# Tile 3's first eight gate and val chunks as half-size products, and a new order of the statements, in an attention and SwiGLU kernel

## The chip, the core and the metric

The kernel runs on one core of a Trainium2 chip. TensorE (PE) multiplies into eight PSUM banks; VectorE (DVE), ScalarE (ACT) and GpSimd (POOL) work on what comes out; SyncE (SP) issues the DMAs. The metric is the device time of one execution in microseconds (us), as the median over runs. The profile of one execution gives the span from the first to the last instruction.

## What is computed

Decayed linear attention over 4 batches, 8 heads, 768 positions and a head size of 64, then a SwiGLU block on the 3072 tokens of width 512, with an inner width of 1536. Inputs and output are float32.

```python
for b in range(nb):
    intra = np.einsum('bhic,bhjc->bhij', qb, kb) * Dmask[None]
    intra = np.einsum('bhij,bhjd->bhid', intra, vb)
    inter = np.einsum('bhid,bhde->bhie', qb * lam_pow[None], kv_state)
    out[:, :, sl] = intra + inter
    kb_dec = kb * rev_pow[None]
    kv_state = lam_block[None, :, None, None] * kv_state + np.einsum('bhsd,bhse->bhde', kb_dec, vb)
...
g = x @ w_gate
silu = g * (1.0 / (1.0 + np.exp(-g)))
val = x @ w_val
return (silu * val @ w_out).astype(np.float32)
```

## The kernel before, in words

The tokens are cut into six tiles (t = 0 to 5) of 512 tokens, each made of two attention groups (g = 2t and 2t + 1) of 256 positions. Matrix products are in bfloat16 with float32 sums.

Attention of a group, in steps: the loads of k, q and v (`load_fp32`, on SP); the casts of k on ACT and the scaling of q on DVE, together `cast_scaled` (L287), which ends in a DMA transpose on SP into `qkt` (L279); the scaling of v (`v_scale`, L266); the scores on PE (L362, from group 6 on L392) and their masks on DVE (L369, L397); the state update `upd_mm` on PE (L424), the copies of its result on ACT (`upd_copy`, L446), and `state`, a chain of additions on POOL (L479) with casts to `kvn` (for groups 8 to 10 on ACT, L459 and L461, taken from a queue by `kv_flush`, L463); then `inter` (L518), a small `guard` copy on ACT, `intra` (L531), and two evacuations into the tile's x, `xt` (L544, L547). These products use 64 rows of the array.

The SwiGLU block of a tile has twelve chunks of 128 inner columns. A chunk (`ffn_fc`) is a gate of four products (L585) and a silu on ACT (L590), then a val of four products (L603) and a multiplication on DVE (L607) that gives the tile's h. Tiles 0 to 3 are done so, with 512 columns in a product, or in halves of 256 where the tile's second group is not there yet (one chunk of tile 0, all of tile 1, four chunks of tile 2).

Tiles 4 and 5 use half-size products in their gate and val instead: `ffn_unit` (L716) takes four chunks (two of each half of the inner width) for all 512 tokens as 2 x 2 blocks and makes them with seven products of blocks in place of eight, each product being four matmuls of 256 columns (L733). It needs sums of weight blocks (`w_combo`, L696), of x blocks (`x_combo`, L714), and copies and additions of partial results: two copies on ACT (L767, L770) and two additions on DVE (L775, L783) for each of gate and val. Four silu and four multiplications (one of them on POOL, L763) finish a unit. The output product does the same from tile 1 on: `out_units` (L805, matmuls L823) makes, with sums of h blocks (`h_combo`, L670) and of w_out blocks (`wo_combo`), two groups' rows in seven products of six matmuls each, called p1 to p7; tile 0 uses the plain `ffn_out` (L623).

The order of the work is what the order of calls in the program says: every engine works through its own queue in that order. Before, a planner writes it: `step` lists the chunks, `at` hangs calls behind a chunk, and the loop at L1184 runs the chunks one by one, between them `run_later` (masks put off), `drip` (one or two sums from the list `trickle`) and `kv_flush`. PSUM banks are taken in a ring by `bank`, unless `fixed` names them. Buffers come from pools with a fixed number of slots (ten of `raw`, three of `qk` and `qkt`, five of `h`, four of `osb`), each free again when its last reader is done.

Of the kernel before, what the change touches and what calls it, by code (L numbers as in the profile page):

```python
# [37 lines left out]
def _body(ctx, tc, nc, q, k, v, lam, moe_w_gate, moe_w_val, moe_w_out, out):  # L38
# [13 lines left out]

    NAT0 = 6
    NB = 4
# [212 lines left out]
    def load_group(g, parts="kqv"):  # L271
        for src, what in ((k, "kraw"), (q, "qraw"), (v, "v")):
            if what[0] in parts:
                load_fp32(g, nc.scalar if what == "kraw" and g in KACT else nc.sync, src, what)

    def dma_transpose(g):
        t = st[("qk", g)]
        tt = qkt_pool.tile([128, 2, 2, HP, 128], BF16, name="qkt", tag="qkt")
        nc.sync.dma_start(out=tt.rearrange("p a s h n -> p (a s h) n"),  # L279
                          in_=t.rearrange("p a s x -> p (a s x)"), transpose=True)  # L280
        st[("qkt", g)] = tt
        for put in held.pop(g, []):
            put()

    QP = ()

    def cast_scaled(g, eng=nc.vector):  # L287
        eng = nc.gpsimd if g in QP else eng
        t = qk_pool.tile([128, 2, 2, H * D], BF16, name="qk", tag="qk")
        st[("qk", g)] = t  # L290
        nc.scalar.copy(out=t[:, 0].rearrange("p s (h d) -> p h s d", h=H),
                       in_=st[("kraw", g)].rearrange("p h (s d) -> p h s d", s=2))
        eng.tensor_tensor(out=t[:, 1].rearrange("p s (h d) -> p h s d", h=H),
                                in0=st[("qraw", g)].rearrange("p h (s d) -> p h s d", s=2),
                                in1=qfac(g), op=ALU.mult)
        dma_transpose(g)
# [38 lines left out]
    KACT = ()  # L335
    HOLD = {(1, 1): 10}
    held = {}
# [6 lines left out]
    def scores(g, cs=(0, 1), warm=0):  # L344
# [9 lines left out]
        for c in cs:  # L354
# [12 lines left out]
            for h2 in range(2):  # L367
                def do_mask(c=c, h2=h2):
                    nc.vector.tensor_tensor(  # L369
                        out=ssb[:, h2, 2 * c:2 * c + 2].rearrange("p a s n -> p a (s n)"),  # L370
                        in0=sp[(c, h2)].rearrange("p (a x) -> p a x", a=2),
                        in1=bap(causal, [[0, 2], [1, 2 * BLK]]),
                        op=ALU.mult)
                later.append(do_mask)
# [5 lines left out]
    def scores_n(g):  # L380
# [14 lines left out]
        for h2 in range(2):  # L395
            def do_mask(h2=h2):
                nc.vector.tensor_tensor(out=ssb[:, h2], in0=sp[h2].rearrange("p (a x) -> p a x", x=M),  # L397
                                        in1=bap(causaln, [[0, 2 * HP], [1, M]]), op=ALU.mult)
            later.append(do_mask)

    def upd(g):
        upd_mm(g)
        upd_copy(g)
        state(g)
# [58 lines left out]
    def kv_flush(age=0, m=9):  # L463
        while kvq and m and len(kvq_now) - kvq[0][0] >= age:
            kvq.pop(0)[1]()
            m -= 1

    def state(g):
# [5 lines left out]
        for n, u in enumerate(us):  # L474
# [9 lines left out]
            elif len(kv) == n + 1:  # L484
                o = kv_pool.tile([128, HP, D], BF16, name="kvn", tag=f"kvn{n}", bufs=2)
                kv.append(o)
                if g in KVA:
                    kvq.append((len(kvq_now), lambda g=g, n=n, o=o, f=f: kv_copy(g, n, o, f, nc.scalar.copy)))
                else:
                    kv_copy(g, n, o, f, nc.gpsimd.tensor_copy)  # L490


# [45 lines left out]
    def evac(g, fns=(nc.scalar.copy, nc.scalar.copy)):  # L538
        op, xt = st[("op", g)], st[("xt", g // 2)]
        for r in range(2):  # L540
            if fns[r] is None:
                continue
            if g < NAT0:
                fns[r](out=xt[:, g % 2, :, r].rearrange("p h (m s) -> p h s m", s=2),  # L544
                       in_=op[r].rearrange("p (h s m) -> p h s m", h=HP, s=2))
            else:
                fns[r](out=bap(xt, [[BLK, 2 * MC], [1, 2], [2, M // 2]], g % 2 * MC * 2 * BLK + r * M),  # L547
                       in_=op[r].rearrange("p (b e x) -> p b e x", b=2 * HP, e=2))

    def core_a(g):  # L550
        kv_flush()
        st[("op", g)] = [bank() for _ in range(2)]
        covered(2 * HP * D, 2)
        inter(g, True)
        guard(g)

    def core_b(g, fns=(nc.scalar.copy, nc.scalar.copy)):
        run_later(len(later))
        intra(g, False)
        evac(g, fns)  # L560

    def core(g, fns=(nc.scalar.copy, nc.scalar.copy)):
        core_a(g)
        core_b(g, fns)

# [4 lines left out]
    HALVED = ((2, 4), (2, 5))  # L570
# [60 lines left out]
    def take(n, seeded, cols):  # L631


        got = [(ring[0] + i) % 8 for i in range(n)]
        ring[0] += n
        yes = [x for x in got if primed[x] >= cols][:len(seeded)]
        assert len(yes) == len(seeded)
        rest = [x for x in got if x not in yes]
        return [yes.pop(0) if i in seeded else rest.pop(0) for i in range(n)]

# [14 lines left out]
    def h_combo(t, j, g=None):  # L655


        fs = slice(0, FH) if g is not None else slice(2 * j[0], 2 * j[1]) if type(j) is tuple else slice(2 * j, 2 * j + 2)
        g0, g1 = (0, B // 2) if g is None else (g, g + 1)
# [3 lines left out]
        for i in range(3):  # L663
            if ("hs", t, i) not in st:
                st[("hs", t, i)] = raw_pool.tile([128, FH, B // 2, BLK], BF16, name="hs", tag="raw")
        s = [st[("hs", t, i)][:, fs, g0:g1] for i in range(3)]
        for o, i0, i1, op in ((s[0], a21, a22, ALU.add), (a21, a11, a21, ALU.subtract),
                              (s[1], s[0], a11, ALU.subtract), (s[2], a12, s[1], ALU.subtract)):
            trickle.append((t, lambda o=o, i0=i0, i1=i1, op=op:
                            nc.vector.tensor_tensor(out=o, in0=i0, in1=i1, op=op)))  # L670

    trickle = []

    def drip(n):
        for _ in range(min(n, len(trickle))):
            trickle.pop(0)[1]()
# [4 lines left out]
    def w_combo(i, n, js=(0, 3)):  # L681
# [14 lines left out]
        nc.vector.tensor_tensor(out=o, in0=i0, in1=i1, op=op)  # L696
# [3 lines left out]
    XS0 = 4  # L700

    def x_combo(t, n, g):
# [6 lines left out]
        if t not in xs:  # L709
            pool, tag = (qkt_pool, "qkt") if t == XS0 else (raw_pool, "raw")  # L710
            xs[t] = pool.tile([128, 3, 2, KH, BLK], BF16, name="xs", tag=tag)
        x = [xs[t][:, m, g] for m in range(3)]
        o, i0, i1 = ((x[0], b12, b11), (x[1], b22, x[0]), (x[2], b21, x[1]), (b12, b22, b12))[n]
        nc.vector.tensor_tensor(out=o, in0=i0, in1=i1, op=ALU.subtract)  # L714

    def ffn_unit(t, j, bk, early=None, mid=None, dr=(0, 0, 2)):  # L716


        xt = st[("xt", t)]
# [3 lines left out]
        hs2 = [st[("h", t, half)][:, 2 * j:2 * j + 2] for half in range(2)]  # L723
# [4 lines left out]
        sil = {}  # L728

        def product(i, o, lhs, rhs, start=False):  # L730
            for fi in range(2):
                for c in range(KH):
                    nc.tensor.matmul(o[:, fi * 256:fi * 256 + 256], lhs(i, c, 2 * j + fi), rhs(c),  # L733
# [556 lines left out]
```

## Time and profile before

| | us |
|---|---|
| median of three runs | 217.0 |
| the three runs | 217.78, 216.41, 217.0 |
| span of the profiled execution | 215.0 |
| PE busy | 208.1 |
| DVE busy | 148.3 |
| ACT busy | 130.9 |
| POOL busy | 92.7 |
| mean of a 512-column product in the row (L585) | 0.380 |
| mean of a 256-column product in the row (L823) | 0.273 |

The profiled execution's own time is not given beside its span. Products overlap in the array, so a row's mean is longer than the step from one product to the next; the chain that ended last shows the steps. L12 stands for line 12 of the kernel. PE, DVE, ACT and POOL busy are unions of their instructions' times.

### The profile page before, as it was taken

Reading aid. Unit: us, or ns where it says so; the run is one execution under the profiler, and the core shown is the slowest. Engines: PE = TensorE matmul, PEld = TensorE weight load, DVE = VectorE, ACT = ScalarE, POOL = GpSimd, SP = SyncE. Lnnn points to the kernel's source line nnn. Section 1 sums busy time; section 2 is a strip of 40 time slices with the busy share of each in tenths; the row PEclk is TensorE's granted clock in tenths of the full one; section 3 lists DMA queues with packets and bytes.
Section 4 is the critical chain, followed back from the end, with each engine's and each line's share of the span. In section 5 each row is a group of like instructions: output and inputs, shape, how many; then the busy total and the mean of one; then the engine's idle time right before and its main releaser. Section 6 shows DMA issues by size and latency. Waiting matters only on the chain.

```text
span 215.0 us, 6856 instructions
## 1 busy us (share of the span) xinstructions
PE 208.1 (97%) x2797; PEld 153.3 (71%) x2801; DVE 148.3 (69%) x267; ACT 130.9 (61%) x280; POOL 92.7 (43%) x128
## 2 busy tenths in 40 slices
PE   8789999999999999999999999999999999999993
PEld 3467445887888548866754545888888888888883
DVE  1773447576677989874569878697988389961940
ACT  5878676756636153638369487774983676636522
POOL 6675755818399440595962153240750022200200
PEclk9999999999999999999999999999999999999999
DMA  6999999999999778899576859855000500005014
GB/s 188 345 354 381 376 336 296 285 226 223 309 387 174 185 212 208 244 214 263 122 198 143 217 121 257 207 121 201 5 3 5 195 0 3 0 0 198 0 52 146
DMA packets 82176, 39.76 MB, mean 185 GB/s; under 512 B 45410, under 2 KB 77794, under 8 KB 82146
## 3 DMA queue, kind: packets, MB, share of 16 engines
q1 hardware_dynamic: 80946, 38.74, 64.7%
q10 hardware_dynamic: 1200, 0.59, 0.9%
q8 instruction: 22, 0.36, 0.7%
q14 instruction: 8, 0.07, 0.1%
HBM read 28.31 MB, written 6.29 MB: 161 GB/s over the span
## 4 chain that ended last, share of the span: by engine, by line
PE 93%; DMA 2%; DVE 1%; SPq 1%; ACT 0%; issue 0%; DVEq 0%
PE bank L823 22%; PE bank L585 20%; PE bank L603 19%; PE bank L733 17%; PE bank L623 5%; PE bank L531 3%; DMA kraw<-in_k_dram 2%; PE bank L518 2%; PE bank L424 2%; PE bank L362 1%; DVE ssb L369 1%; SPq L115 1%; PE bank L392 1%; PE bank L322 1%; ACT qk L306 0%
## 5 line engine op out<-in xcount | busy, mean ns | idle before, releaser
L607 DVE TENSOR_TENSOR h<-sil,bank 128x256 bf16<-128x256 bf16 (+1 forms) x67 | 35.0, 533 | 29.9 <-PE bank L603 17.2
L585 PE MATMUL bank<-xt,wg_sb 128*128 128x256 bf16 (+1 forms) x276 | 52.8, 315 | 0.0
L603 PE MATMUL bank<-xt,wv_sb 128*128 128x256 bf16 (+1 forms) x276 | 52.5, 314 | 0.0
L590 ACT ACTIVATE sil<-bank 128x256 bf16<-128x256 f32 (+1 forms) x67 | 31.6, 481 | 21.8 <-PE bank L585 18.4
L603 PEld LDWEIGHTS <-wv_sb 128*128 128x128 bf16 x276 | 26.9, 98 | 14.8 <-POOL wv_sb L249 0.2
L585 PEld LDWEIGHTS <-wg_sb 128*128 128x128 bf16 x276 | 25.9, 98 | 13.6 <-issue 0.2
L266 POOL TENSOR_TENSOR v_s<-v,dec 128x512 bf16<-128x512 f32 (+1 forms) x18 | 23.0, 1295 | 24.3 <-DMA v<-in_v_dram 17.3
L763 POOL TENSOR_TENSOR h<-sil,es 128x512 bf16<-128x512 bf16 x6 | 7.0, 1165 | 47.4 <-ACT sil L760 47.4
L823 PEld LDWEIGHTS <-h 128*128 128x128 bf16 x240 | 23.3, 98 | 3.4 <-issue 0.3
L823 PE MATMUL bank<-wo_sb,h 128*128 128x256 bf16 x180 | 21.5, 273 | 0.0
L823 PEld LDWEIGHTS <-hs 128*128 128x128 bf16 x180 | 17.6, 98 | 2.7
L369 DVE TENSOR_TENSOR ssb<-bank,causal 128x512 bf16<-128x512 f32 x24 | 15.4, 684 | 1.8 <-PE bank L362 1.8
L479 POOL TENSOR_TENSOR kvf<-kvs,ups 128x256 f32<-128x256 f32 x8 | 6.5, 814 | 20.9 <-ACT ups L446 20.9
L733 PEld LDWEIGHTS <-ws 128*128 128x128 bf16 x144 | 13.8, 98 | 1.8
L823 PE MATMUL bank<-wt,hs 128*128 128x256 bf16 x120 | 15.0, 273 | 0.0
L775 DVE TENSOR_TENSOR bank<-bank,es 128x512 f32<-128x512 f32 x12 | 7.8, 694 | 9.6 <-PE bank L733 9.6
L479 POOL TENSOR_TENSOR kvf<-kvf,ups 128x256 f32<-128x256 f32 x16 | 13.0, 815 | 0.9
L760 ACT ACTIVATE sil<-bank 128x512 bf16<-128x512 f32 x18 | 10.5, 596 | 3.7 <-PE bank L733 3.7
L733 PE MATMUL bank<-xs,ws 128*128 128x256 bf16 x96 | 12.6, 273 | 0.0
L763 DVE TENSOR_TENSOR h<-sil,bank 128x512 bf16<-128x512 bf16 x18 | 11.8, 683 | 0.3 <-ACT sil L760 0.3
L623 PE MATMUL bank<-wo_sb,h 128*128 128x512 bf16 x45 | 10.7, 380 | 0.2
L733 PE MATMUL bank<-xt,wg_sb 128*128 128x256 bf16 x72 | 10.8, 273 | 0.0
(119 smaller groups left out, 360.3 us busy)
## 6 DMA issues: line engine op xcount, KB each, us to landing
out_dram<-osb SPq DMA_DIRECT2D x22, 256.0 KB, 2.6
v<-in_v_dram SPq DMA_DIRECT2D x18, 256.0 KB, 4.6
woraw<-in_moe_w_out_dram SPq DMA_DIRECT2D x6, 512.0 KB, 7.1
kraw<-in_k_dram SPq DMA_DIRECT2D x24, 128.0 KB, 3.4
qraw<-in_q_dram SPq DMA_DIRECT2D x24, 128.0 KB, 3.4
wraw<-in_moe_w_gate_dram SPq DMA_DIRECT2D x5, 512.0 KB, 6.9
wraw<-in_moe_w_val_dram SPq DMA_DIRECT2D x5, 512.0 KB, 7.0
kraw<-in_k_dram SPq DMA_DIRECT2D x4, 512.0 KB, 6.3
```

Of the source, the lines that this page charges most:

```text
L266: eng.tensor_tensor(out=st[("vs", g)][:, h0:h1], in0=st[("v", g)][:, h0:h1].rearrange("p h (s d) -> p h s d", s=2), in1=vfac(g, h0, h1), o ...
L369: nc.vector.tensor_tensor(out=ssb[:, h2, 2 * c:2 * c + 2].rearrange("p a s n -> p a (s n)"), in0=sp[(c, h2)].rearrange("p (a x) -> p a x", ...
L479: nc.gpsimd.tensor_tensor(out=o, in0=f, in1=u, op=ALU.add)
L585: nc.tensor.matmul(gp[:, n0:n1], wg_sb[:, mc, fs], xt[:, g0:g1, mc].rearrange("p g b n -> p g (b n)"), start=(mc == 0 and n0 == 0), stop=( ...
L590: nc.scalar.activation(sil[:, 0:N], gp[:, 0:N], AF.Silu)
L603: nc.tensor.matmul(vp[:, n0:n1], wv_sb[:, mc, fs], xt[:, g0:g1, mc].rearrange("p g b n -> p g (b n)"), start=(mc == 0 and n0 == 0), stop=( ...
L607: nc.vector.tensor_tensor(out=h_sb[:, fc % FH, b0:b1].rearrange("p b n -> p (b n)"), in0=sil[:, 0:N], in1=vp[:, 0:N], op=ALU.mult)
L623: nc.tensor.matmul(ps, st[("h", t, fc // FH)][:, fc % FH, b], wo_sb[:, fc, c0:c1], start=(fc == 0), stop=(fc == FC - 1))
L733: nc.tensor.matmul(o[:, fi * 256:fi * 256 + 256], lhs(i, c, 2 * j + fi), rhs(c), start=(start and fi == 0 and c == 0), stop=(c == KH - 1), ...
L760: nc.scalar.activation(sil[key], src, AF.Silu)
L763: eng.tensor_tensor(out=h_of(half, r), in0=v3(sil[half, r]), in1=v3(src), op=ALU.mult)
L823: nc.tensor.matmul(o, lhs(f), rhs(f), start=(start and f == 0), stop=(f == FH - 1), skip_group_check=True)
```

## The change

Of tile 3's twelve chunks, chunks 0 to 3 and 6 to 9 are made in two units of seven half-size products, as in tiles 4 and 5; chunks 4, 5, 10 and 11 stay as they were. Tile 3 gets four sums of x for that (the last of them into a place of its own, `xsum(3)`, so that x itself stays whole for the plain chunks).

The order is written out as a flat list of statements from `ffn_gate(0, 2)` on; what stands ahead of that is as before. The planner, `trickle`, `drip`, `kv_flush` and the ring's use from there on are gone: `use` names the banks of each statement. The helpers are taken apart so that each statement is one step: `kcast`, `qcast` and `dma_transpose` for `cast_scaled`; `mask` for a put-off mask; `kvc` for a put-off state cast; `evr` for one evacuation; `hsum(t, k, ...)` for one of the four sums of h; `unit` and `uprod(t, j, k, i)` (product k of 0 to 6, i = 0 gate, 1 val), `silu` and `mu` for `ffn_unit`; `out_new`, `oprod(t, g, k)` and `store` for `out_units`. A gate and its val no longer follow each other always; masks, casts, sums, loads and stores stand in other places; some sums, casts and scalings move from DVE or ACT to POOL (an argument `nc.gpsimd` or `POOLC`), some v scalings from POOL to DVE. Two of tile 2's chunks that are made in pieces by group are now 10 and 11, no longer 4 and 5, and the four that are made in halves are 6 to 9, no longer 0 to 3.

```diff
+    def kcast(g, fn=nc.scalar.copy):
+        fn(out=qk_new(g)[:, 0].rearrange("p s (h d) -> p h s d", h=H),
+           in_=st[("kraw", g)].rearrange("p h (s d) -> p h s d", s=2))
+
+    def qcast(g, eng=nc.vector):
+        eng.tensor_tensor(out=qk_new(g)[:, 1].rearrange("p s (h d) -> p h s d", h=H),
+                          in0=st[("qraw", g)].rearrange("p h (s d) -> p h s d", s=2),
+                          in1=qfac(g), op=ALU.mult)
...
+    def hsum(t, k, f0, f1, g0=0, g1=2, eng=None):
...
+        o, i0, i1, op = ((s[0], a21, a22, ALU.add), (a21, a11, a21, ALU.subtract),
+                         (s[1], s[0], a11, ALU.subtract), (s[2], a12, s[1], ALU.subtract))[k]
+        (eng or nc.vector).tensor_tensor(out=o, in0=i0, in1=i1, op=op)
...
-    HALVED = ((2, 4), (2, 5))
+    HALVED = ((2, 10), (2, 11))
...
-    XS0 = 4
+    XS0 = (3, 4)
...
+            xs[t] = pool.tile([128, 4 if t == 3 else 3, 2, KH, BLK], BF16, name="xs", tag=tag)
+        x = [xs[t][:, m, g] for m in range(4 if t == 3 else 3)]
+        o, i0, i1 = ((x[0], b12, b11), (x[1], b22, x[0]), (x[2], b21, x[1]),
+                     (x[3] if t == 3 else b12, b22, b12))[n]
...
+        o, lhs, rhs = ((A, wa(0, 0), xb(0, 0)), (E, wa(0, 1), xsum(3) if t == 3 else xb(0, 1)), (Bb, wsum(1), xsum(1)),
+                       (A, wa(1, 0), xb(1, 0)), (Bb, wsum(0), xsum(0)), (E, wa(1, 1), xsum(2)),
+                       (Bb, wsum(2), xb(1, 1)))[k]
+        for fi in range(2):
+            for c in range(KH):
+                nc.tensor.matmul(o[i][:, fi * 256:fi * 256 + 256], lhs(c, 2 * j + fi), rhs(c),
...
+        if k == 0:
+            nc.scalar.copy(out=Bb[i], in_=A[i])
+        if k == 1:
+            nc.scalar.copy(out=es[i], in_=E[i])
+        if k == 2:
+            nc.vector.tensor_tensor(out=E[i], in0=Bb[i], in1=es[i], op=ALU.add)
+        if k == 4:
+            nc.vector.tensor_tensor(out=es[i], in0=Bb[i], in1=es[i], op=ALU.add)
...
+    use(0); ffn_gate(0, 9, 0, 4)
+    use(1); ffn_val(0, 7, 0, 4)
...
+    use(2); ffn_val(0, 8, 0, 4)
+    use(4, 5); pe_transpose(2, 0)
+    use(6, 7); pe_transpose(2, 1)
+    w_cast()
...
+    use(1); ffn_val(0, 9, 0, 4)
+    use(2, 3, 0, 5); scores(2)
...
+    use(6); ffn_gate(0, 10, 0, 4)
...
+    use(4, 5); upd_mm(3)
...
+    upd_copy(3)
+    use(6); ffn_gate(1, 8, 0, 2)
+    use(7); ffn_val(1, 8, 0, 2)
+    use(4); ffn_gate(1, 9, 0, 2)
...
+    use(0, 1); scores(8)
+    guard(7)
+    upd_copy(8)
+    intra(7, False)
+    evr(7, 1, ACTC)
+    use(2); ffn_gate(2, 5, 0, 4)
+    state(8)
+    w_combo(1, 3, (0, 2))
+    evr(7, 0, DVEC)
+    mask(8, 0, 0)
+    hs_new(2)
+    x_combo(3, 0, None)
+    mask(8, 0, 1)
+    x_combo(3, 3, None)
+    use(7); ffn_val(2, 5, 0, 4)
+    x_combo(3, 1, None, nc.gpsimd)
+    hsum(2, 0, 0, 4, 0, 2)
+    new_xt(4)
+    unit(3, 0, (0, 1, 5, 3, 4, 2))
+    uprod(3, 0, 0, 0)
+    uprod(3, 0, 0, 1)
+    kvc(8, 1)
+    uprod(3, 0, 1, 0)
+    uprod(3, 0, 3, 0)
+    x_combo(3, 2, None, nc.gpsimd)
+    uprod(3, 0, 2, 0)
...
+    intra(8, False)
+    state(9)
+    qcast(10, nc.vector)
+    mask(9, 0, 0)
+    use(7); ffn_val(3, 4, 0, 4)
+    dma_transpose(10)
+    store(1, 1, 1, 0, 512, None)
+    store(1, 1, 0, 0, 512, None)
...
+    mu(5, 1, 0, 1)
+    hsum(5, 2, 0, 2, 0, 2)
+    hsum(5, 1, 0, 2, 0, 2)
+    hsum(5, 3, 0, 2, 0, 2)
+    hs_new(5)
+    out_new(4, (0, 1), [7, 0, 3, 5, 2, 1], 256)
+    oprod(4, 1, 1)
+    oprod(4, 0, 1)
+    hsum(5, 0, 2, 4, 0, 2)
+    oprod(4, 0, 7)
+    oprod(4, 1, 7)
+    hsum(5, 2, 2, 4, 0, 2)
+    mu(5, 1, 1, 0)
+    oprod(4, 0, 6)
+    hsum(4, 3, 0, 2, 0, 2, nc.gpsimd)
+    hsum(5, 1, 2, 4, 0, 2, nc.gpsimd)
+    oprod(4, 1, 6)
+    oprod(4, 0, 2)
+    oprod(4, 1, 2)
+    oprod(4, 0, 5)
```

More of the change, by code (lines that the diff above doesn't have):

```diff
@@ L395, in scores_n @@
         for h2 in range(2):
[L396 to L404, printed above, removed]
+            st[("sp", g, 0, h2)] = sp[h2]
+            later.append(lambda h2=h2: mask(g, 0, h2))
     def upd_mm(g, up=None):
```

1217 lines of the change are left out of this document (763 added, 454 removed).

## The prediction

> **What bounds the kernel now.** I read the page's busy shares and clock first, then the chain that ended last, the waits of TensorE, and at last the stretch that the change makes denser.
>
> ```profile
> span 215.0 us, 6856 instructions
> ...
> PE 208.1 (97%) x2797; PEld 153.3 (71%) x2801; DVE 148.3 (69%) x267; ACT 130.9 (61%) x280; POOL 92.7 (43%) x128
> ...
> PEclk9999999999999999999999999999999999999999
> ...
> PE 93%; DMA 2%; DVE 1%; SPq 1%; ACT 0%; issue 0%; DVEq 0%
> ```
>
> TensorE (PE) is busy 97% at full clock, and 93% of the chain is PE. Busy alone does not prove that PE streams at its rate; the chain in order of time does:
>
> ```profile
> 27.18 0.86 PE bank L603 x4
> 28.05 0.86 PE bank L585 x4
> ...
> 97.47 0.38 PE bank L518 x32
> 98.11 0.32 PE bank L392 x31
> 98.43 0.32 PE bank L531 x32
> 98.75 0.97 PE bank L585 x4
> 99.71 0.86 PE bank L603 x4
> ...
> 135.39 9.17 PE bank L823 x84
> ```
>
> Four 512-column products take 0.86 us every time; 84 products of 256 columns take 9.17, 0.109 each, with nothing between. A chunk behind an attention stretch takes 0.97: leaving the 64-row products costs 0.11. The waits of PE in the whole run:
>
> ```profile
> PE bank L188 <- PEq L1274: 0.8, 1, 0.8
> PE bank L322 <- ACT qk L306: 0.7, 2, 0.4
> PE bank L362 <- DVE qkt L328: 0.5, 1, 0.5
> PE bank L362 <- ACT qkt L324: 0.3, 1, 0.3
> PE bank L518 <- ACT guard L502: 0.3, 1, 0.3
> PE bank L531 <- issue: 0.3, 1, 0.3
> PE bank L362 <- ACT ups L446: 0.2, 1, 0.2
> ```
>
> All but the 0.3 behind the guard lie ahead of tile 0's third chunk, so in unchanged code. A new order has therefore almost nothing to win (0.3 us) and much to lose: only fewer PE columns make this kernel faster.
>
> **The change, term by term.** The sum is made on the profiled span, 215.0. The profiled execution's own time is not given beside it; the median of three runs is 217.0, so I add 2.0 at the end.
>
> *Products.* Eight chunks of tile 3, gate and val, four products each: 64 products of 512 columns leave, 16 x 0.86 = 13.8 us. Two units of 14 half-size products come, 112 matmuls of 256 columns at 9.17/84: 12.2 us. Net -1.55 us. Nothing hides this; it is the whole gain.
>
> *Attention stretches.* PE's order shows 27 separate runs of 64-row products in place of 26. One more costs 0.11 behind it and about as much ahead: +0.2.
>
> *Work on the other engines.* Each unit adds four ACT copies (0.574 and 0.612) and four DVE adds (0.694 and 0.685), and tile 3 four sums of x. In exchange the new order gives POOL three query scalings (1.91 each in the POOL row), ten sums of h or parts of them, four sums of x, one key cast, one piece of a weight sum, and two multiplications from the units; DVE gets five half-group v scalings. Queue lists times the shortest row of each kind: DVE 154.6 to 156.1, ACT 143.5 to 144.3, POOL 86.3 to 107.4. So no engine overtakes PE over the whole span, and what matters is where the extra lies. From unit(3,0) to tile 3's last val the statements give PE 28 x 0.437 + 8 x 0.863 + 2.8 of attention = 21.9 us. ACT has ten kvn copies (0.40), two key casts (1.05), eight unit copies, eight silu (0.60), four chunk silu (0.60), four ups copies, two xt copies (0.76), two guards: 21.9 us of durations; over the whole run busy over summed durations is 130.9/143.5, so about 19.9 busy. POOL has 16.8. The same length before:
>
> ```profile
> core 0: us, PE busy (x) PEld busy (x) DVE busy (x) ACT busy (x) POOL busy (x), PEclk, DMA share, GB/s
> ...
> 112.00:134.00 22.00, 22.00 (x331) 10.98 (x330) 19.20 (x29) 15.79 (x33) 7.82 (x10) 1.00 0.75 183
> ```
>
> ACT goes from 72% to some 91% and POOL from 36% to 76%, DVE stays (19.0 summed). Covers there become thin. Stalls are priced at the hand-overs where a queue's ledger comes out near PE's (none can be below 0, since PE has no wait at these places now):
>
> *(a) gate(0,10).* Its weights are cast on ACT behind the four copies of group 2's transposes:
>
> ```profile
> 32.06 1.14 ACT L324 COPY qkt<-bank 128x512 bf16<-128x512 bf16 x2 [0.79 <-PE bank L322]
> 33.10 1.05 ACT L249 CAST wg_sb<-wraw 128x1024 bf16<-128x1024 f32 x1
> ```
>
> The transposes began at 31.50, the cast ended 2.65 later, and this gate began 3.38 after them. The new order puts gate(0,9) ahead of the transposes, so PE comes 0.86 earlier: 2.52 against 2.65 and a hand-over. Stall 0.2; bounds 0 and 0.86.
>
> *(b) Entry into tile 3's units.* With intra(7) done, PE has gate(2,5), val(2,5) and one product: 0.11 + 0.86 + 0.86 + 0.44 = 2.3. The next product takes scores(8)'s second bank, and ahead of its mask DVE has evr(7,0) 0.73, a mask 0.69, a sum of x 0.42, then that mask 0.69; neighbours overlap by 0.08 in the rows (w_combo(1,3) ahead of them is hidden by the attention stretch), and 0.2 is the last matmul's own length: 2.5. So 0.2. Two products later the sums of x on POOL are due, behind state(8)'s three adds (0.72), and then the adds into Bb behind a 0.68 sum of h. I take 0.8 for the whole entry; bounds 0 and 2.7 (0.2 and three POOL instructions of 0.72, 0.72 and 1.05 in DVE's way).
>
> *(c) Tile 4's output units.* Behind the last product of unit (5,1), DVE has a silu to wait for (0.8), two multiplications (0.68), five sums of h (0.42) and the add (0.43) before oprod(4,0,5) may write: 4.1 with overlaps. PE comes after eight products of 0.655, 5.2. Slack 1.1, but POOL runs three instructions of over 1 us on the same tiles. I take 0.4; bounds 0 and 2.2 (three times 1.1, less the slack).
>
> *(d) Smaller ones.* gate(1,9) takes a bank of upd_mm(3), whose three ACT copies need 1.15 against two chunks, 1.0: 0.15. intra(5) stands behind four masks that follow three weight sums: 0.15. Bounds 0 and 0.6.
>
> Moved DMAs: a group's loads still follow the transpose of the group ahead on SP. A transpose takes 3.7 us to land (142.13 to 145.86; PE used it at 146.31). In the new order the thinnest is group 10's, with 4.9 us of products from intra(8), where its scaling stands on DVE, to its scores: 0; bounds 0 and 1.2, the scaling's own row. Two stores of tile 1 now wait behind that transpose on SP; their osb buffers are due at tile 2's output, some 7 us later, against 2.6 to landing: 0; bounds 0 and 2.6.
>
> What the collisions of (b) and (c) are, the trace shows at 77 us:
>
> ```profile
> 77.39 2.64 POOL L266 TENSOR_TENSOR v_s<-v,dec 128x1024 bf16<-128x1024 f32 x1 [5.27 <-DMA v<-in_v_dram]
> ```
>
> ```profile
> 77.06 1.20 DVE L293 TENSOR_TENSOR qk<-qraw,qdn 128x1024 bf16<-128x1024 f32 x1
> 78.18 2.27 DVE L670 TENSOR_TENSOR hs<-h 128x768 bf16<-128x768 bf16 x1
> 80.48 0.56 DVE L670 TENSOR_TENSOR h<-h 128x768 bf16<-128x768 bf16 x1
> ```
>
> POOL waited for DVE's scaling (2.64 instead of 1.91), then DVE's sum waited until POOL was done (2.27 instead of 0.55). The Trainium skill, "SBUF — State Buffer", section "Who interferes with whom", states this as a rule: a DVE instruction with two SBUF inputs contends with a GpSimd instruction that reads SBUF, and whoever starts first holds the shared port for the whole instruction. By that rule, which the trace bears out here, moving sums to POOL speaks against the change; were the ports free, (c) would be 0.
>
> Sum: -1.55 + 0.2 + 0.2 + 0.8 + 0.4 + 0.3 = +0.35. Span 215.35, time 217.4.
>
> **Rivals.**
>
> *R1, the covers hold.* DVE was full before (150 to 155 us) and PE did not stop, so thin covers can hold. Then only -1.55 + 0.2 remain: span 213.65, time 215.6. Against it: ledgers (a) and (b) come out short with no collision at all.
>
> *R2, slower: ACT becomes the bound of tile 3's 22 us.* Place: from unit(3,0) to val(3,11). Half of a unit's products wait for ACT copies, and behind the first 20 us no stretch of this length had ACT over some 75%. If its neighbours do not overlap, because each waits for its own PE product, the 21.9 us of durations count in full, and its 40 hand-overs at about 0.1 us each come on top: 4.0 us of stall, with 1.0 elsewhere. Span 215.0 - 1.35 + 5.0 = 218.65, time 220.65. It decides from 3.55 us of stalls in all: with 1.0 elsewhere, from about 0.065 us for each hand-over. Against it: kvn copies and key casts have slack.
>
> *R3, the DVE and POOL collisions reach PE everywhere.* POOL's 21 us more are 11% of the 190 us; some 65 DVE instructions with two SBUF inputs meet it, and half of a POOL row (1.2) is a mean wait of 0.6: 65 x 0.11 x 0.6 = 4.3 us. With 0.7 us of (a), (d) and the collision-free part of (b): span 213.65 + 5.0 = 218.65, time 220.65. Against it: before, waits of this kind (1.7 us at 78) did not stop PE.
>
> **How the numbers follow.** Faster or slower means over 1% (2.2 us), about what a measurement of this kernel can tell from none. Forecast 0.60, its own range 216.2 to 218.6 (stalls of 0.5 to 3); R1 0.18, R2 0.12, R3 0.10. Faster needs more than the products' whole gain: 0.05, from R1 and the runs' spread (216.4 to 217.8). Slower: four fifths of R2, two thirds of R3, a little of the forecast, 0.19. Same is the rest, 0.76. The range reaches to R1 below with the spread and most of the way to R2 above: 215.3 to 219.6.
>
> **What would show it.** Right: unit rows at 0.109 a product, about 12.2 us for tile 3's 112; PE's waits naming DVE or POOL at tile 3's entry, and ACT's cast at gate(0,10); the stretch's windows near ACT 19.9 and POOL 16.8. R1: no PE waits beyond those of before. R2: PE waiting for unit copies, ACT full there. R3: DVE sums of over 1 us against 0.42. The forecast is wrong if a store or transpose lands late, or if stalls sum to under 0.5 or over 3 us.

## The result

The changed kernel took 217.59 us (median of 22 executions, 217.27 to 219.52), the kernel before 216.87 beside it (22 executions, 216.14 to 218.44). The ratio is 1.0045, with an interval of 1.003 to 1.0059: half a per cent slower, within the 1% that was forecast as most likely, and 0.2 us above the time named. The forecast added 0.35 to a base of 217.0; measured are 0.72 on 216.87. The page of the profile after, whose lines answer to those of before:

```profile
span 215.7 us, 6968 instructions
...
PE 207.0 (96%) x2845; PEld 157.8 (73%) x2849; DVE 151.4 (70%) x267; ACT 132.0 (61%) x283; POOL 117.4 (54%) x145
...
PE 89%; DVE 3%; DMA 2%; ACT 2%; SPq 1%; issue 1%; ACTq 0%; DVEq 0%
```

PE has 48 products more, since 64 wide ones became 112 narrow ones, and is busy 1.1 us less. What it lost is the chain's share: 93% was PE, now 89%, and DVE went from 1% to 3%, ACT from under 1% to 2%. So PE now stands behind other engines. Line numbers are those of the changed kernel: L715 is a unit's product, L774 an output product, L559 a gate, L577 a val, L358 a mask, L679 a sum of x, L632 a sum of h, L723 and L725 a unit's adds, L734 its silu, L740 its multiplication; L347 are scores, L500 and L513 the inter and intra products. PE's waits in the whole run (us in total, times, longest):

```profile
...
PE bank L715 <- DVE ssb L358: 0.4, 1, 0.4
PE bank L513 <- DVE ssb L362: 0.4, 1, 0.4
PE bank L347 <- ACT qkt L312: 0.3, 1, 0.3
PE bank L500 <- ACT guard L484: 0.3, 1, 0.3
PE bank L513 <- issue: 0.3, 1, 0.3
PE bank L347 <- ACT ups L430: 0.2, 1, 0.2
PE bank L559 <- ACT wg_sb L243: 0.2, 1, 0.2
```

The first and the last of these are new beside the list of before; that of L513 for a mask lies in the head, in unchanged code. They are the two places that the prediction named as (b) and (a). The view shows only where PE stood still; with start-to-start times of the products the losses (the excess over the steady step from product to product) come out whole: gate (0,10) 0.30 us, gate (1,9) 0.26, at tile 3's entry 0.59 and 0.26, and in unit (3,1) 0.15, in all 1.56. Two smaller ones in tile 5's units, 0.14 at 178.46 and 0.16 in place of 0.10 at 184.76, are made up for elsewhere. The chain of waits in order of time shows the entry (start, us, what):

```profile
110.36 0.74 DVE xt L531
111.09 0.06 DVE ssb L358
111.16 0.43 issue
111.58 0.51 DVE xs L679
112.09 0.07 issue
112.16 0.69 DVE ssb L358
112.89 2.39 PE bank L715 x20
115.30 0.59 ACT es L721
115.92 0.71 DVE bank L723
116.67 8.60 PE bank L715 x76
```

DVE does a copy, a mask, a sum of x and the second mask in a row, and the product at 112.89 waits for the last: this is the 0.59. The chain then follows five products of four matmuls to ACT's copy and DVE's add, for which the product at 116.67 waits: this is the 0.26. Ahead of that add DVE was idle for 0.24 us, so this second wait is not DVE's queue but the way from a product over a copy and an add to the next product. In the 76 matmuls behind it lies the 0.15.

Where the end came: PE's last product started at 211.40 us before and at 211.39 after. So in these two executions all that the products gave (1.55 us) was spent on waits, and the 0.7 us between the spans lies behind PE's last product. No term of the prediction stood for that, so the experiments begin there.

### The profile page after: what moved, and what is told of

Same layout as the page of the kernel before. It is cut to its first block, busy times and chain, and to the rows that moved or that the text cites. A ratio compares the mean times of both kernels' runs of the same rounds, so it can differ in the third digit from the quotient of the medians.

```text
span 215.7 us, 6968 instructions
## 1 busy us (share of the span) xinstructions
PE 207.0 (96%) x2845; PEld 157.8 (73%) x2849; DVE 151.4 (70%) x267; ACT 132.0 (61%) x283; POOL 117.4 (54%) x145
## 4 chain that ended last, share of the span: by engine, by line
PE 89%; DVE 3%; DMA 2%; ACT 2%; SPq 1%; issue 1%; ACTq 0%; DVEq 0%
PE bank L715 22%; PE bank L774 21%; PE bank L559 16%; PE bank L577 15%; PE bank L597 5%; PE bank L513 3%; DMA kraw<-in_k_dram 2%; PE bank L500 2%; PE bank L408 1%; DVE ssb L362 1%; PE bank L347 1%; SPq L109 1%; PE bank L310 1%; PE bank L383 1%; ACT wg_sb L243 0%
## 5 line engine op out<-in xcount | busy, mean ns | idle before, releaser
L581 DVE TENSOR_TENSOR h<-sil,bank 128x256 bf16<-128x256 bf16 (+1 forms) x59 | 29.6, 513 | 20.7 <-PE bank L577 14.8
L559 PE MATMUL bank<-xt,wg_sb 128*128 128x256 bf16 (+1 forms) x244 | 42.1, 306 | 0.3 <-ACT wg_sb L243 0.2
L577 PE MATMUL bank<-xt,wv_sb 128*128 128x256 bf16 (+1 forms) x244 | 42.3, 306 | 0.0
L564 ACT ACTIVATE sil<-bank 128x256 bf16<-128x256 f32 (+1 forms) x59 | 26.8, 465 | 20.3 <-PE bank L559 16.0
L559 PEld LDWEIGHTS <-wg_sb 128*128 128x128 bf16 x244 | 22.9, 98 | 10.7 <-ACT wg_sb L243 0.4
L577 PEld LDWEIGHTS <-wv_sb 128*128 128x128 bf16 x244 | 23.4, 98 | 9.7
L740 POOL TENSOR_TENSOR h<-sil,es 128x512 bf16<-128x512 bf16 x8 | 9.7, 1210 | 35.0 <-ACT sil L734 33.7
L774 PEld LDWEIGHTS <-h 128*128 128x128 bf16 x240 | 23.4, 98 | 3.9 <-issue 0.3
L260 POOL TENSOR_TENSOR v_s<-v,dec 128x512 bf16<-128x512 f32 (+1 forms) x14 | 17.6, 1275 | 8.1 <-DMA v<-in_v_dram 3.7
L774 PE MATMUL bank<-wo_sb,h 128*128 128x256 bf16 x180 | 22.0, 273 | 0.0
L715 PEld LDWEIGHTS <-ws 128*128 128x128 bf16 x192 | 18.7, 98 | 3.0 <-issue 0.6
L774 PEld LDWEIGHTS <-hs 128*128 128x128 bf16 x180 | 17.6, 98 | 2.8
L723 DVE TENSOR_TENSOR bank<-bank,es 128x512 f32<-128x512 f32 x16 | 10.7, 697 | 12.6 <-PE bank L715 10.5
L715 PE MATMUL bank<-xs,ws 128*128 128x256 bf16 x128 | 17.7, 272 | 0.1
L740 DVE TENSOR_TENSOR h<-sil,bank 128x512 bf16<-128x512 bf16 x24 | 15.6, 681 | 1.5 <-ACT sil L734 1.5
L734 ACT ACTIVATE sil<-bank 128x512 bf16<-128x512 f32 x24 | 13.5, 593 | 3.5 <-PE bank L715 3.4
L774 PE MATMUL bank<-wt,hs 128*128 128x256 bf16 x120 | 15.3, 272 | 0.0
L715 PEld LDWEIGHTS <-wv_sb 128*128 128x128 bf16 x128 | 12.3, 98 | 2.1 <-issue 0.6
L715 PEld LDWEIGHTS <-wg_sb 128*128 128x128 bf16 x128 | 12.5, 98 | 1.7 <-DVE ssb L358 0.2
L715 PE MATMUL bank<-xt,wv_sb 128*128 128x256 bf16 x88 | 13.1, 273 | 0.4 <-DVE ssb L358 0.4
```

The costliest lines, as they stand in the source:

```text
L260: eng.tensor_tensor(out=st[("vs", g)][:, h0:h1], in0=st[("v", g)][:, h0:h1].rearrange("p h (s d) -> p h s d", s=2), in1=vfac(g, h0, h1), o ...
L559: nc.tensor.matmul(gp[:, n0:n1], wg_sb[:, mc, fs], xt[:, g0:g1, mc].rearrange("p g b n -> p g (b n)"), start=(mc == 0 and n0 == 0), stop=( ...
L564: nc.scalar.activation(sil[:, 0:N], gp[:, 0:N], AF.Silu)
L577: nc.tensor.matmul(vp[:, n0:n1], wv_sb[:, mc, fs], xt[:, g0:g1, mc].rearrange("p g b n -> p g (b n)"), start=(mc == 0 and n0 == 0), stop=( ...
L581: nc.vector.tensor_tensor(out=h_sb[:, fc % FH, b0:b1].rearrange("p b n -> p (b n)"), in0=sil[:, 0:N], in1=vp[:, 0:N], op=ALU.mult)
L715: nc.tensor.matmul(o[i][:, fi * 256:fi * 256 + 256], lhs(c, 2 * j + fi), rhs(c), start=(k < 2 and fi == 0 and c == 0), stop=(c == KH - 1), ...
```

## Experiments

Each kernel was timed in five rounds beside the kernel before. The stretch is PE's time from the first product of unit (3,0) to the first of tile 2's output; "landed" is the time from the start of PE's last product to the moment when SP has seen the last store land. Both are from one traced execution. The runs are numbered as the expectations count them.

| kernel | stretch | PE's last product | landed | median us | ratio to before |
|---|---|---|---|---|---|
| before | - | 211.40 | 2.69 | 216.87 | 1 |
| changed | 23.16 | 211.39 | 3.05 | 217.59 | 1.0045 (1.003 to 1.0059) |
| e1 stores as before | 23.18 | 211.76 | 2.66 | 217.66 | 1.004 (1.0017 to 1.0063) |
| e2 before, new stores | - | 211.36 | 3.07 | 217.15 | 1.0025 (1.0003 to 1.0047) |
| e3 mask first | 23.28 | 211.53 | 3.06 | 217.56 | 1.0051 (1.0032 to 1.007) |
| e4 gates | 23.02 | 212.35 | 3.05 | 218.00 | 1.0061 (1.0042 to 1.0081) |
| e5 plain chunks | - | 212.61 | 3.06 | 218.12 | 1.0057 (1.0035 to 1.0079) |
| e6 more ACT | 24.17 | 212.36 | 3.04 | 218.72 | 1.0077 (1.0051 to 1.0102) |
| e7 sums on DVE | 24.38 | 213.83 | 3.93 | 221.05 | 1.0209 (1.0156 to 1.0262) |
| e8 e1 + e3 + e4 | 23.14 | 211.22 | 2.65 | 217.44 | 1.0032 (1.0006 to 1.0058) |
| e9 queue reordered | 23.17 | 211.64 | 3.04 | 217.56 | 1.0034 (1.0007 to 1.0062) |
| e10 e9 + e1 + gates | 23.01 | 210.67 | 2.65 | 217.81 | 1.0045 (1.0015 to 1.0076) |
| e11 e9, two sums later | 23.32 | 212.12 | 3.05 | 217.93 | 1.0059 (1.0036 to 1.0082) |
| e12 e11 + e10 | 23.33 | 211.90 | 2.65 | 217.48 | 1.0037 (1.0016 to 1.0059) |

### The closing stores: e1 and e2

```
     oprod(5, 0, 4)
     store(5, 0, 1, 0, 512, None)
-    oprod(5, 0, 3)
     oprod(5, 1, 4)
     store(5, 1, 1, 0, 512, None)
+    oprod(5, 0, 3)
     store(5, 0, 0, 256, 512, None)
     oprod(5, 1, 3)
```

> The changed kernel, with its last output rows in the order of the kernel before: product 4 and its store for group 0, the same for group 1, then product 3 of group 0 with its store, then product 3 of group 1. Theory (the closing stores cost what the PE stalls do not): PE's last product ends at about 211.7 in both kernels, and the 0.7 us between the spans lies behind it, because the store of the second half of row 0 stands behind a 256 KB store on SP (issued at 211.83, not at about 211.45). Expected: PE's end unchanged at 211.7, that store about 0.4 earlier, span 215.0 to 215.3, ratio to the kernel before 1.000 to 1.003. Rival (the end differs by chance from one execution to the next, and the loss lies in stalls ahead): span 215.7, ratio about 1.0045.

e2 makes the opposite edit in the kernel before:

```
-        run(ps[:n])
+        run(ps[:5] if last else ps[:n])
+        if last:
+            p4(0)
+            p3(0)            # its store is taken out of p3
+            p4(1)
+            store(0, 0, HD, DM)
+            p3(1)
```

> The kernel before, with the last output rows in the order of the changed kernel (product 3 of group 0 ahead of product 4 of group 1, its store behind the next one). Theory of the closing stores: span 0.4 to 0.7 longer, 215.4 to 215.7, ratio to the kernel before 1.002 to 1.003. Rival (chance): 1.000.

The DMA view of the last 9 us gives, for each kind of store, the bytes and the median time from issue to landing. The changed kernel:

```profile
out_dram<-osb SPq DMA_DIRECT2D x1, 128.0 KB, 2.0
out_dram<-osb ACTq DMA_DIRECT2D x1, 64.0 KB, 2.1
out_dram<-osb SPq DMA_DIRECT2D x1, 64.0 KB, 2.0
```

e1, with the stores as before (the kernel before shows the same three numbers):

```profile
out_dram<-osb SPq DMA_DIRECT2D x1, 128.0 KB, 1.7
out_dram<-osb ACTq DMA_DIRECT2D x1, 64.0 KB, 1.7
out_dram<-osb SPq DMA_DIRECT2D x1, 64.0 KB, 1.6
```

In the new order SP issues its second 256 KB store, the 128 KB store and the last 64 KB store at 211.44, 211.83 and 212.34, ACT its own at 212.00; before, SP's second 256 KB store left at 210.79 and the 128 KB store at 211.45. So the last four now leave within 0.9 us, and the three small ones take 0.3 to 0.4 us longer to land. The "landed" column is as steady as a price can be: 2.65 to 2.69 in all traces with the old order, 3.04 to 3.07 with the new one (e7 apart, whose stores left at the same distances, but whose last one took 0.9 longer to land). So the order of the closing stores costs 0.38 us, in both kernels. Timing agrees for e2 (+0.46 in the medians of its rounds, 217.15 against 216.69, and the interval leaves out 1). It does not for e1: the ratio stayed at 1.004, as the rival had it, and the traced execution had PE 0.37 later from a wait at 59 us, in code that the edit does not touch. The rest of the 0.7 between the spans lies in the closing steps, from the last landing that SP sees to the last instruction: 0.87 us before, 1.29 in the changed kernel, 0.83 to 1.28 in the others. Most of it stands at one place, between two of GpSimd's closing steps: 0.44 us in the changed kernel's trace, 0.13 before; 0.42 or more came in four of the fourteen traces, 0.13 in the others, and kernels with either order of stores are in both sets. So it does not go with the stores. Whether it is chance, one trace of each kernel cannot tell; since the medians of 22 executions lie 0.72 apart as well, some 0.3 us beyond the stores stays open.

### Products against stalls: e5

The two units are undone, all else stays: 16 gate and val products of tile 3 as before, no sums of x, the two pieces of the weight sums behind them.

```
-    unit(3, 0, (0, 1, 5, 3, 4, 2))
-    uprod(3, 0, 0, 0)
...
+    use(5); ffn_gate(3, 0, 0, 4)
+    use(3); ffn_val(3, 0, 0, 4)
...
+    w_combo(0, 3, (0, 2))
+    w_combo(1, 3, (0, 2))
```

> The changed kernel, with the products of the change alone undone: tile 3's chunks 0 to 3 and 6 to 9 as plain gate and val chunks (16 of four products of 512 columns) in place of two units, its four sums of x left out, the two pieces of the gate and val weights' sum in place moved behind them. Theory: +1.55 for the products, less the stalls of the units (0.59 at the entry, 0.26 and 0.15 inside): about +0.6 us on the changed kernel, 218.2, ratio to the kernel before 1.007. If the units' stalls are all there is to lose in this stretch, PE's stretch from the end of the last attention run of group 7 to tile 2's output grows by 0.5 to 0.8. Rival R2 or R3 (ACT bound or collisions from the units' extra work all over the stretch): the plain chunks take that load away and gain 1 us or more somewhere else: at most 217.0.

The median rose by 0.5 us (218.12 against 217.59; the intervals overlap), of which 0.2 lies outside the profiled span: the time exceeds the span by 1.97 us on average in e5 and by 1.77 in the changed kernel. The trace says it more sharply, for one execution of each: from tile 1's last output products to tile 2's first, PE took 30.13 us with chunks (106.11 to 136.24) and 29.64 with units (105.39 to 135.03). So the units gain 0.49 of their 1.55 and lose 1.06 to waits, in which the 1.00 counted above is found again. Why they wait, the stretch from 112 to 134 us shows. With the units:

```profile
112.00:134.00 22.00, 21.48 (x380) 15.58 (x377) 18.70 (x30) 17.83 (x36) 18.65 (x16) 1.00 0.78 192
```

With plain chunks in the same order of all else (columns as in the prediction's view: PE, weight loads, DVE, ACT, POOL):

```profile
112.00:134.00 22.00, 22.00 (x216) 10.13 (x214) 14.81 (x24) 13.70 (x27) 13.12 (x12) 1.00 0.72 176
```

To save 1.55 us of PE the units put some 4 us more on DVE (14.81 to 18.70), 4 on ACT and 5.5 on POOL into the same 22 us. The same figures say what the rest of the new order costs: e5 has before's products and is 1.3 us slower than before (218.12 against 216.78 in its rounds). Gates (0,10) and (1,9) with 0.56 and the stores with 0.38 are 0.94 of that; another 0.25 lies outside the span, where the kernel before has 1.72.

### The entry: e3, e9 and e11

```
     evr(7, 0, DVEC)
     mask(8, 0, 0)
+    mask(8, 0, 1)
     hs_new(2)
     x_combo(3, 0, None)
-    mask(8, 0, 1)
     x_combo(3, 3, None)
+    x_combo(3, 1, None)
     use(7); ffn_val(2, 5, 0, 4)
-    x_combo(3, 1, None, nc.gpsimd)
```

> The changed kernel, with the second mask of group 8 ahead of the first sum of x on DVE, and the sum x1 of tile 3 on DVE instead of POOL. Theory (term b): the second product of unit (3,0) no longer waits (its excess of 0.59 us falls under 0.1), and the saving reaches the end: PE's last product at about 211.1, span about 215.1, time 0.6 us below the changed kernel's (ratio to the kernel before 1.001 to 1.003). Rival 1: x1 or the adds into the banks are late in their turn, the product five places on waits 0.4 to 0.6 and the time does not move. Rival 2: a later stage is bound by DVE, and tile 2's output begins 0.6 earlier but PE's last product still ends at 211.7.

The theory fell, and the time did not move, as rival 1 had it: the product that had waited 0.59 ran on, and the very next one, not the one five places on, waited 0.69, for x3 instead. PE's waits of e3 from 104 to 136 us:

```profile
PE bank L715 <- DVE xs L679: 0.5, 1, 0.5
```

e9 puts all of DVE's queue there in PE's order and moves the copies and adds of the unit as well:

```
+    mask(8, 0, 0)
     evr(7, 0, DVEC)
+    mask(8, 0, 1)
     hs_new(2)
+    x_combo(3, 3, None)
     x_combo(3, 0, None)
+    x_combo(3, 1, None)
...
     uprod(3, 0, 1, 0)
+    uprod(3, 0, 1, 1)
     x_combo(3, 2, None, nc.gpsimd)
     uprod(3, 0, 2, 0)
+    uprod(3, 0, 2, 1)
+    kvc(8, 1)
     uprod(3, 0, 3, 0)
```

> The changed kernel, with DVE's queue at tile 3's entry put in the order in which PE needs it: the first mask of group 8 ahead of the copy of group 7's output (the scores end 0.3 us before that copy can start), then the second mask, then x3, x0 and x1, all three on DVE; and unit (3,0)'s products in the order of tile 4's units, products 1 and 1 ahead of 2 and 2, with one copy of a state moved behind the two copies that the adds wait for. Theory after the third run (DVE's queue ahead of PE's third product, five instructions in a row, is the limit, and moving one mask only moved the wait): the excess at the entry, 0.59 in the changed kernel and 0.69 in the third run, falls to 0.1, the 0.26 further on to 0.1 as well: PE reaches tile 2's output 0.6 to 0.8 earlier, span about 0.7 below the changed kernel's, ratio to the kernel before about 1.001. Rival (the units' adds and copies are the limit, whatever the order): the waits appear again within unit (3,0), sum over 0.6.

Again the rival: the entry is free (excess under 0.1), and the fifth pair of products waits 0.69 and 0.16 for DVE's adds. DVE in e9 (start, us):

```profile
112.08 1.28 DVE L679 TENSOR_TENSOR xs<-xt 128x512 bf16<-128x512 bf16 x2
113.39 0.42 DVE L679 TENSOR_TENSOR xs<-xt,xs 128x512 bf16<-128x512 bf16 x1
113.74 0.68 DVE L581 TENSOR_TENSOR h<-sil,bank 128x512 bf16<-128x512 bf16 x1
114.33 1.32 DVE L632 TENSOR_TENSOR hs<-h 128x1024 bf16<-128x1024 bf16 x1
115.58 1.28 DVE L723 TENSOR_TENSOR bank<-bank,es 128x512 f32<-128x512 f32 x2
```

Its neighbour POOL:

```profile
111.44 1.64 POOL L462 TENSOR_TENSOR kvf<-kvf,ups 128x256 f32<-128x256 f32 x2
113.95 1.16 POOL L679 TENSOR_TENSOR xs<-xt,xs 128x512 bf16<-128x512 bf16 x1 [0.87 <-ACT bank L719]
115.07 2.35 POOL L282 TENSOR_TENSOR qk<-qraw,qdn 128x1024 bf16<-128x1024 f32 x1
```

Two sums of x took 1.28 us, the second of them held up until POOL's adds ended at 113.08, where the one after them, alone, took 0.42. The sum of h took 1.32 beside POOL's sum of x; of its size, 0.68 is seen where POOL starts behind it (in the changed kernel at 117.97). Against two sums at 0.42 that overlap by 0.08, and one at 0.68, some 1.1 us of DVE's queue here is waiting for POOL. e11 takes the sum of h, and the one behind it, out of the adds' way:

```
-    hsum(2, 0, 0, 4, 0, 2)
     new_xt(4)
...
-    hsum(2, 1, 0, 4, 0, 2)
...
     mu(3, 0, 1, 0)
     mu(3, 0, 0, 0)
+    hsum(2, 0, 0, 4, 0, 2)
+    hsum(2, 1, 0, 4, 0, 2)
```

> The kernel of the ninth run (DVE's queue at the entry in PE's order), with the sum of h for tile 2's output that stands on DVE ahead of unit (3,0)'s adds, and the one behind it, moved behind that unit's multiplications; the output needs them some 15 us later. Theory: the wait of 0.6 to 0.8 us that moved through three places when single instructions were moved is DVE's queue as a whole, lengthened by POOL (that sum took 1.32 us beside a POOL sum of 1.16, the sums of x 0.65 in place of 0.42); with 1.3 us less of DVE work ahead of the adds it ends: the waits of 0.69 and 0.16 at the unit's fifth pair of products fall to 0.2 together, and PE reaches tile 2's output 0.6 to 0.8 earlier in the stretch (23.2 us from the unit's first product in the run before, 22.5 here). Rival (the adds wait for ACT's copies, or PE's later waits take it back): the stretch stays at 23.2.

Unit (3,0) now runs without a wait, and unit (3,1) waits 1.29 us behind the two sums. PE's waits of e11 from 104 to 136:

```profile
PE bank L715 <- DVE bank L723: 1.1, 1, 1.1
PE bank L774 <- DVE bank L783: 0.6, 1, 0.6
```

and DVE in front of that wait:

```profile
118.53 1.29 DVE L740 TENSOR_TENSOR h<-sil,bank 128x512 bf16<-128x512 bf16 x2 [0.58 <-ACT sil L734]
119.73 1.08 DVE L632 TENSOR_TENSOR hs<-h 128x1024 bf16<-128x1024 bf16 x1
120.84 1.42 DVE L632 TENSOR_TENSOR h<-h 128x1024 bf16<-128x1024 bf16 x1
122.19 1.28 DVE L723 TENSOR_TENSOR bank<-bank,es 128x512 f32<-128x512 f32 x2
```

Four orders of the same work, four places of the wait, and the stretch stays between 23.2 and 23.3 us, where PE's work alone is 22.2 (23.16 less the waits of 1.00). The rival of e11 came too. What the four traces show together fits DVE's load in the stretch, with POOL's collisions in it, better than any one hand-over, but it is read from the traces and not isolated by a run. That no order is better was not shown; four were tried.

### ACT and POOL: e6 and e7

e6 does the key casts of groups 9 and 10 twice:

```
     kcast(9)
+    kcast(9)
...
     kcast(10)
+    kcast(10)
```

> The changed kernel, with the key casts of groups 9 and 10 done twice on ACT (the second overwrites the first with the same values): 2.1 us more of ACT inside tile 3's stretch. Theory: ACT has some 4 us idle there (17.8 of 22.0 busy), so at most 0.3 us reaches PE. Rival R2 (ACT near its bound in this stretch): 1 to 2 us, time 218.6 to 219.6.

This one was a miss for the theory. The stretch grew from 23.16 to 24.17, and the median from 217.59 to 218.72: half of the 2.1 us reached PE, although ACT seemed to have 4 us idle. PE's waits in e6 from 104 to 136:

```profile
PE bank L715 <- DVE ssb L358: 0.4, 1, 0.4
PE bank L715 <- ACT sil L734: 0.4, 1, 0.4
```

and ACT ahead of the second:

```profile
115.74 2.13 ACT L278 CAST qk<-kraw 128x1024 bf16<-128x1024 f32 x2
117.77 0.59 ACT L734 ACTIVATE sil<-bank 128x512 bf16<-128x512 f32 x1
118.26 0.62 ACT L734 ACTIVATE sil<-es 128x512 bf16<-128x512 f32 x1
118.78 1.07 ACT L734 ACTIVATE sil<-bank 128x512 bf16<-128x512 f32 x2
```

Unit (3,1) needs the bank that the third silu reads, and the 1.05 us of cast more ahead of it became 0.57 us at this product; the second cast cost 0.29 at a val further on. So the mechanism of R2 is there; in the change itself its price was not.

e7 puts back on DVE every sum that stands on POOL (15 lines like this):

```
-    hsum(2, 2, 0, 4, 0, 2, nc.gpsimd)
+    hsum(2, 2, 0, 4, 0, 2)
```

> The changed kernel, with every sum that stands on POOL (of h, of x, one piece of a weight sum: 15 statements) on DVE instead; scalings, casts and multiplications stay on POOL. Theory (the covers held, and the collisions of DVE with POOL cost PE little): PE gains nothing from fewer collisions, and loses where DVE's queue comes out short, in tile 4's and tile 3's units: 0 to +2 us. Rival R3 (collisions reach PE): each DVE instruction is no longer held up by a POOL sum, 0.5 us or more faster: 217.0 or less.

It is 3.5 us slower than the changed kernel, more than either theory said. In its trace PE's last product comes 2.44 later, and 0.9 more is the late landing of its last store, whose cause is open. PE's waits in e7 from 104 to 136:

```profile
PE bank L500 <- DVE h L740: 1.2, 1, 1.2
PE bank L715 <- DVE ssb L358: 0.4, 1, 0.4
```

Group 8's inter products wait for a multiplication that now stands behind two sums of h. The first of these took 1.64 us beside a multiplication that stays on POOL, so this wait is in part a collision too. e7 shows that this order pays more with the sums on DVE than on POOL; it does not show what the collisions cost.

### The gates: e4, and three versions with several repairs: e8, e10, e12

```
     use(6, 7); pe_transpose(2, 1)
-    w_cast()
+    w_cast((DVEC, POOLC))
...
-    use(4); ffn_gate(1, 9, 0, 2)
+    use(1); ffn_gate(1, 9, 0, 2)
```

> The changed kernel, with the cast of the last gate weights (chunks 10 and 11) on DVE instead of ACT, and gate (1,9) in a bank whose mask is long done instead of a bank of the update of group 3. Theory (terms a and d): gate (0,10) loses its excess of 0.30 us and gate (1,9) its 0.26, PE's later work comes 0.5 us earlier and stays so: span about 215.2, ratio to the kernel before 1.001 to 1.003. Rival: the masks of group 2, behind the cast on DVE, or the scores of group 3, bound by their transpose on SP, take the time back, and PE is at the same place as before by tile 1's second half: no change.

Gate (1,9) lost its 0.26. Gate (0,10) went the wrong way, from 0.30 to 0.66: the cast met POOL. e4:

```profile
33.89 2.50 POOL L260 TENSOR_TENSOR v_s<-v,dec 128x512 bf16<-128x512 f32 x2
34.14 1.35 DVE L243 CAST wg_sb<-wraw 128x1024 bf16<-128x1024 f32 x1
```

e8 has the same edit, but in its execution a load landed later, and POOL began behind the cast's start:

```profile
33.90 0.68 DVE L243 CAST wg_sb<-wraw 128x1024 bf16<-128x1024 f32 x1
34.39 1.08 POOL L243 CAST wv_sb<-wraw 128x1024 bf16<-128x1024 f32 x1 [2.76 <-DMA wraw<-in_moe_w_val_dram]
```

The same cast took 1.35 us where POOL had started 0.25 ahead of it and 0.68 where it had not. The Trainium skill, "SBUF — State Buffer", section "Who interferes with whom", says that casts too can enter a mode in which DVE contends with GpSimd, and that whoever issues first blocks the other for the whole instruction. e4's trace agrees: POOL's first scaling ended at 34.94 and DVE's cast, alone 0.68 long, at 35.49, and POOL's second scaling took 1.50 in place of 1.04. In e8 POOL's cast, behind DVE's, took 1.08 in place of 1.04, so there a hold-up hardly shows. Gate (0,10) had no excess left there. As a whole e4 came out no faster than the changed kernel (ratio 1.0061), so its theory fell.

> The changed kernel, with three edits together: the closing stores in the order of the kernel before, the mask and x1 at tile 3's entry, and the cast and the bank ahead of gates (0,10) and (1,9). Theory (each loss is its own and the saving stays): 0.5 + 0.6 + 0.5 = 1.6 us below the changed kernel, about 216.0, ratio to the kernel before 0.996. Rival (later hand-overs take the time back): only the closing stores' 0.5 remains, ratio about 1.002.

e10 keeps that cast on ACT, in two halves of 128 columns, beside e9's order, gate (1,9)'s bank and the stores of before:

```
-    w_cast()
+    wg10, wg10r = w_raw.pop(0)
+    for c in range(2):
+        ACTC(out=wg10[:, :, c * 128:c * 128 + 128], in_=wg10r[:, :, c * 128:c * 128 + 128])
+    w_cast((POOLC,))
```

> The edits of the run before, with the closing stores in the order of the kernel before, gate (1,9) in its other bank, and the cast of the last gate weights left on ACT but in two halves, so that gate (0,10) waits for the first half only (0.6 instead of 1.05 us). Theory: 0.7 + 0.5 + 0.26 + 0.3 = 1.8 us below the changed kernel, about 215.8, ratio to the kernel before 0.995. Rival (part of the saving goes to waits further on, as in the runs of the single edits): ratio 0.998 to 1.002.

> The same, with the edits of the tenth run: closing stores in the order of the kernel before, gate (1,9) in its other bank, and the cast ahead of gate (0,10) in two halves. Theory: PE's work from end to end 0.8 + 0.56 shorter and the end 0.4, so the fastest execution falls to 215.4 to 215.8 and the median to 216.6 to 217.0, level with the kernel before (ratio 0.998 to 1.002); the spread of the tenth run (2.7 us) stays, since it comes from loads that land at other times. Rival: the median stays at 217.6 or above, and then PE's earlier arrival is lost to those loads in most executions.

In e10's trace both gates are free of excess, and PE's last product starts at 210.67, 0.7 earlier than before, with a span of 214.4. But its twelve executions have spans of 214.4 to 217.1, and the median is 217.81. e8 and e12 come to 217.44 and 217.48. The theories of a full 1.6 to 1.8 us fell: 0.1 of it shows in the medians of e8 and e12, well inside their intervals, and none in e10's. Of what is missing, 0.17 us lies outside the span (1.94 to 1.95 in these three against 1.77); the median spans of e8 and e12 are 215.5 against 215.8. What else takes the time back in the executions without a trace is open. Two traces show one way. In e12's, a load of q landed at 44.40 us (42.34 in the changed kernel's); DVE's scaling of it started at 44.49 (42.77), the multiplications of h stood behind it, and a val of tile 1 waited 0.58 us for one of them. In e5's the same load landed at 44.89, and the val waited 0.40. So the loads that e12's expectation names can cost PE this much; how often they do, no run shows. The traces also differ as a whole: up to tile 1's last output products, the changed kernel, e1, e3, e6, e9 and e11 have the same statements, and they reach that point between 105.35 (e6) and 105.92 us (e11); the 0.6 us wait at L774 in e11's view above, one of these statements, is in none of the others. No version beat the kernel before.

## Why the prediction was right, step by step

- *Products, -1.55.* Right: the 112 matmuls take 0.109 each, and no product of the units is slower apart from its waits. In e5 the stretch gets longer by that sum less the units' waits, 0.49.
- *One more attention stretch, +0.2.* Not told apart; the switches cost 0.09 into and 0.11 to 0.14 out of 64-row products, as before.
- *(a) gate (0,10), 0.2.* 0.30, and behind ACT's cast, as the wait says. Halving the cast removes it (e10).
- *(b) tile 3's entry, 0.8.* 0.85: 0.59 at the instruction that was named (the second mask), where the account as a ledger of DVE's queue was right, and 0.26 at an add, which was named too, but which stood behind ACT's copy and not behind the sum of h. The 0.15 in unit (3,1) was in no term. What the account did not see is that a wait of this size comes back in all of the orders tried.
- *(c) tile 4's output units, 0.4.* Nothing: the slack of 1.1 us held.
- *(d) 0.3.* 0.26, all of it gate (1,9); intra (5) did not wait.
- *Moved DMAs, 0.* The step that was mis-sized. The text weighed loads, transposes and two stores of tile 1, and left out the stores that close the kernel, where no PE work covers a store: +0.38 (e1 and e2). A store that lands late was one of the forecast's own signs of being wrong.

Taken together the stalls came to 1.56 where 1.7 were forecast. So the mechanism was right where PE works, thinner covers eating the products' gain; that the time named lies so near the measured one is in part luck. 0.4 too much for (c) stands against 0.38 missing for the stores; the change as such, 0.72, is twice the 0.35 forecast, with some 0.3 open; and the base, a median of three, was 0.13 above that of 22. The 2.0 added for the time outside the span measured 1.72 to 1.77, and the span 215.7, not 215.35.

Of the rivals, R1 failed at (a), (b) and (d). R2's mechanism is there, but the change stops short of it: ACT was busy 17.83 of the 22 us and not 19.9, because two copies of updates and both copies of group 9's output (2.1 us) fell behind 134.0. e6 shows that 2.1 us more would have begun to cost. POOL came out the other way, 18.65 against 16.8: its sums of x took 1.48 each beside DVE and its first multiplication 1.48, where 1.16 is seen elsewhere. R3 did not spread: in the changed kernel a collision stands ahead of a wait of PE only at the entry, where a sum of x took 0.65 in place of 0.42. In e4, e7, e9 and e11 collisions lengthen the waits too.

## What to carry to other kernels

A trade that frees the bounding engine at the price of the others is worth what the stretch allows in which it is made: here 1.55 us of PE were bought with 4 to 5.5 us on each of three engines that were at 60 to 67% there, and in the traces a third of it was left. When a wait moves to the next hand-over as soon as one is repaired, compare the queue's whole load in the stretch, collisions included, before another order is tried. And treat the stores behind the last product as a path of their own: no PE work covers them here, and their order cost as much as a stall (0.38 us).

## What was not expected of the hardware

- The order of five closing stores is worth 0.38 us, the same to 0.04 in thirteen of fourteen traces: when the last four leave within 0.9 us, the three small ones take 2.0 to 2.1 us to land and not 1.6 to 1.7.
- A kernel's time exceeds its span by an amount of its own: 1.72 us on average for the kernel before, 1.77 for the changed one, and 1.94 to 1.97 for e1, e5, e8, e10 and e12. In e1 this is 0.19 us, half of what its stores saved. Its cause is open.
- Executions of the same statements differ by up to 0.57 us at the same product, halfway through. A gain of 0.5 us is safe to read in these traces only stretch by stretch; in the medians of 6 to 12 executions it is not.
